# Row norms on VectorE, 24 weight pieces in attention instead of 30, and the first piece loads spread over the loop

## The chip, the cores and the metric

The kernel runs on one core of one Trainium2 chip. The metric is the time of one execution on the device, in microseconds (us). A profiled execution of the same program gives the trace that is read below.

## The reference

Three layers follow one another. Attention has 4 batches, 12 heads, 448 positions and 64 dimensions per head, and uses a sigmoid in place of a softmax. Its output, 1792 rows of 768, goes through a mixture of 8 experts in which each row takes one expert: the choice needs the norm of each row. The last layer multiplies two projections elementwise and projects back.

```python
scores = scale * np.matmul(q, k.transpose(0, 1, 3, 2)) - np.log(S)
x = rows of np.matmul(1.0 / (1.0 + np.exp(-scores)), v)          # 1792 x 768

xn = x / (np.linalg.norm(x, axis=-1, keepdims=True) + 1e-06)
logits = xn @ en.T / tau                                         # 8 experts
expert_idx = np.argmax(logits, axis=1)
out[row] = gate_w[row] * (relu(x[row] @ w1[e]) @ w2[e])          # e = expert_idx[row]

y = (out @ w_a) * (out @ w_b) @ w_out                            # w_a, w_b: 768 x 1536
```

## The kernel before, in words

**Attention** runs over 24 pairs of heads, six per batch, in a software pipeline. Iteration i of the loop (L596) transposes the queries and keys of pair i + 1 on TensorE and splits them into a high and a low part (`tr_pair`: L524 on ScalarE, L525 on VectorE), computes the scores of pair i (L538) with the sigmoid on ScalarE (L539), and multiplies by the values for pair i - 1 (`av_part`, L550). At the end of `av_part` VectorE copies the result to `xT` (L554); this copy also frees the only PSUM buffer of its kind. GpSimd then squares the pair (L559, L562) and adds the square to a sum per batch, `xsq` (L563). `x_tok` (L566) turns pair i - 2 back to rows of tokens: four transposes on TensorE (L573), a copy on VectorE (L574), and after each third pair a store of the rows (L577) on SP's queue.

After a batch's sixth pair `route(b)` is put in a list of background jobs. It multiplies `xT` by the normed expert embeddings `enT` and, in the same group of matmuls, `xsq` by a matrix `sqT` that sums over partitions (L248); ScalarE copies the result (L250), and L254 adds the four quarters with a matrix `sum9`, eight columns for the logits and a ninth for the sum of squares. VectorE takes the ninth as `ss` (L260), and `inv_norm` computes the inverse norm, mostly on GpSimd. `head` (L667) loads tau and the embeddings, norms them and writes `enT`; it is a background job too. `pump` advances one such job by one step (up to its next `yield`), and each iteration has four calls of it. A job that yields True waits for a call that may use PSUM.

**Weight pieces.** The weights of the last layer are made from integer reads of `w_a`, `w_b` and `w_out` in 72 units, six per block f of 128 hidden columns (`prep_load` and `prep_unit`). A unit is 128 x 384: two VectorE instructions (L198, L200), two of ScalarE (L202 and L204, which writes the buffer `ab`), one of GpSimd (L205), and a last one of VectorE (L215). Units of attention are stored to the scratch `wm` (L227). `prep_tick` (L229) stores what is finished, finishes what waits (all but `behind` units), loads the unit three ahead, and starts one unit. There are three buffers `ab`, two `m` and four `raw`. In attention there is one tick at the end of each of the 24 iterations and an extra one with behind=1 in every fourth, so that `6 * F_EARLY` = 30 units are done there. All loads and stores named here are on SP's queue, which issues in program order.

**Experts.** 18 live blocks of 128 rows go through `w1` and `w2`; no unit of weights is made there until its end.

**Last stage** (`glu`). Four groups of up to 512 rows, twelve blocks f each, make 48 steps. Step i first splits the weights of step i + 1 (`w_split`), multiplies (`ab`, L1037 to L1039, with the product of the two projections at L1045 on VectorE), and adds the output of step i - 1. Blocks below `F_EARLY` are loaded from the scratch `wm`; the other blocks of the first group are made in place, with four ticks in even steps and five in odd ones (`prep_more`), and `w_split` forces further ticks while its block lacks units:

```python
while F_EARLY <= i < NF and wr_n.get(i, 0) < 6:
    prep_tick()
```

Of the kernel before, what the change touches and what calls it, by code (L numbers as in the profile page):

```python
# [9 lines left out]
F32 = mybir.dt.float32  # L10
# [5 lines left out]
ALU = mybir.AluOpType  # L16
# [8 lines left out]
def build(ctx: ExitStack, tc: tile.TileContext, q, k, v, emb, tau, w1, w2, wa, wb, wo, out, dbg=None, stop=None):  # L25
# [6 lines left out]
    nc = tc.nc  # L32
    B, H, S, D = q.shape
    E, DM = emb.shape
    DF = w1.shape[2]
    DF2 = wa.shape[1]
    P = 128
    NCH = 4
    CP = S // NCH
    NP = H // 2  # L40
# [3 lines left out]
    HD = DM // 2  # L44
# [28 lines left out]
    def ctile(shape, nm, dt=F32):  # L73
        return const.tile(shape, dt, name=nm, tag=nm)

    ident = ctile([P, P], "ident")
# [11 lines left out]
    bias_s = ctile([P, 1], "bias_s")  # L88
    tau_r = ctile([P, 1], "tau_r")
    enT = ctile([P, KD, 32], "enT")  # L90
    sqT = ctile([P, 32], "sqT")
    sum9 = ctile([P, E + 1], "sum9")
    oh_all = ctile([CP, B * NCH, E], "oh_all")
    rk_all = ctile([CP, B * NCH], "rk_all")
    run = ctile([P, E2], "run")
# [6 lines left out]
    def constants():  # L102
        gp = nc.gpsimd

        def iota(t, pattern, base=0, cm=0):
            gp.iota(t, pattern=pattern, base=base, channel_multiplier=cm, allow_small_or_imprecise_dtypes=True)

        make_identity(nc, ident)
        gp.tensor_copy(out=ident_r, in_=ident)
        gp.memset(bias_s, -math.log(S))  # L110
        gp.memset(enT, 0.0)
        gp.memset(sqT, 0.0)
        gp.memset(sqT[:, E:E + 1], 1.0)
        gp.memset(ones, 1.0)
        gp.affine_select(out=tri, in_=ones, pattern=[[1, P]], compare_op=ALU.is_gt, fill=0.0, base=0,
                         channel_multiplier=-1)
        gp.memset(tri16, 1.0)
        gp.affine_select(out=tri16, in_=tri16, pattern=[[1, E2], [-1, E2]], compare_op=ALU.is_ge, fill=0.0, base=0,
                         channel_multiplier=0)
        iota(iota8m, [[1, E]], base=-E)  # L120
        iota(iota128, [[1, P]])
        iota(ids, [[S, B], [1, NCH]], cm=NCH)
        n0 = len(PHASES[0]) * NCH
        iota(yrow[:, :n0], [[S, len(PHASES[0])], [1, NCH]], base=Y0 + 1, cm=NCH)
        iota(yrow[:, n0:], [[S, len(PHASES[1])], [1, NCH]], base=1, cm=NCH)
        iota(pads, [[P, NBLK]], base=CAP[1] + 1, cm=1)
        iota(blk_i, [[1, NBLK + 1]])
        iota(blk_128, [[P, JMAX]])
        gp.memset(run, 0.0)
        gp.memset(last3, -1.0)  # L130
        gp.tensor_tensor(out=sum9, in0=ident[:, 0:E + 1], in1=ident[:, 32:32 + E + 1], op=ALU.add)
        for g in (2, 3):
            gp.tensor_tensor(out=sum9, in0=sum9, in1=ident[:, 32 * g:32 * g + E + 1], op=ALU.add)

    def inv_norm(ss, rows, cols, tag, eng, res):

# [27 lines left out]

    HU = DM // 2
    units = [(f, part, hf) for f in range(NF) for part in range(3) for hf in range(2)]
    F_EARLY = 5
    next_unit, unit_end = [0], [6 * F_EARLY]
    prep_raw = {}

# [64 lines left out]

    misc = {}
    LATE, END = "late", "end"
    xT, xsq, xtok = {}, {}, {}

    def route(b):  # L240
        ph = phase_of[b]
        c0 = b * NCH

        pl = misc["ps"]()
        ops = [(enT[:, hp, :], xT[b, hp]) for hp in range(NP)] + [(sqT, xsq[b])]
        for i, (l, r) in enumerate(ops):
            g = 32 * (i % 4)
            nc.tensor.matmul(pl[g:g + 32, :S], lhsT=l, rhs=r, start=i < 4, stop=i + 4 >= len(ops))  # L248
        lT = misc["xp"].tile([P, S], F32, tag="lT", name="lT", bufs=1)
        nc.scalar.copy(out=lT, in_=pl[:, :S])  # L250
        yield True
        ps = misc["ps"]()
        for c in range(NCH):
            nc.tensor.matmul(ps[:CP, c * (E + 1):(c + 1) * (E + 1)], lhsT=lT[:, c * CP:(c + 1) * CP], rhs=sum9,  # L254
                             start=True, stop=True)
        ls = small.tile([CP, NCH, E + 1], F32, tag="ls", name="ls")
        nc.vector.tensor_copy(out=ls, in_=ps[:CP, :NCH * (E + 1)].rearrange("p (c e) -> p c e", c=NCH))
        misc[f"logits{b}"] = True
        ss = small.tile([CP, NCH], F32, tag="ss", name="ss")
        nc.vector.tensor_copy(out=ss, in_=ls[:, :, E])  # L260
        res = []
        gp = nc.gpsimd
        yield from inv_norm(ss, CP, NCH, "x", gp, res)
# [4 lines left out]

        ve = nc.vector
        l0 = st("l0")  # L270
        ve.tensor_tensor(out=l0, in0=ls[:, :, :E], in1=rn.unsqueeze(2).to_broadcast([CP, NCH, E]), op=ALU.mult)
        l1 = st("l1")
        ve.tensor_scalar(out=l1, in0=l0, scalar1=tau_r[:CP], scalar2=None, op0=ALU.mult)
        mx = st("mx", (CP, NCH))
# [193 lines left out]
    def attention():  # L468
# [73 lines left out]
        def av_part(i, half):  # L542
            if half == 0:
                av[i] = ps_a.tile([P, 512], F32, tag="av", name="av")
            t = av[i]
            a = A.pop((i, half))
            for c2 in range(2):
                c = 2 * half + c2
                for j in range(2):
                    nc.tensor.matmul(t[j * D:(j + 1) * D, :S], lhsT=raw[i, "v"][:, j, c, :], rhs=a[:, c2, j, :],  # L550
                                     start=c == 0, stop=c == NCH - 1)
            if half == 1:
                x = xT_p.tile([P, S], F32, tag="xT", name="xT", bufs=NP + 1)
                nc.vector.tensor_copy(out=x, in_=t[:, :S])  # L554
                xT[pairs[i]] = x
                b, hp = pairs[i]
                if hp == 0:
                    xsq[b] = xT_p.tile([P, S], F32, tag="xsq", name="xsq", bufs=2)
                    nc.gpsimd.tensor_tensor(out=xsq[b], in0=x, in1=x, op=ALU.mult)  # L559
                else:  # L560
                    x2 = xT_p.tile([P, S], F32, tag="x2", name="x2", bufs=1)
                    nc.gpsimd.tensor_tensor(out=x2, in0=x, in1=x, op=ALU.mult)  # L562
                    nc.gpsimd.tensor_tensor(out=xsq[b], in0=xsq[b], in1=x2, op=ALU.add)  # L563
                del av[i]

        def x_tok(i):  # L566
            b, hp = pairs[i]
            if hp == 0:
                xtok[b] = misc["xp"].tile([CP, NCH, DM], F32, tag="xtok", name="xtok", bufs=1)
            pm = misc["ps"]()  # L570
            pmv = pm[:CP].rearrange("p (c d) -> p c d", c=NCH)
            for c in range(NCH):
                nc.tensor.transpose(out=pmv[:, c, :], in_=xT[b, hp][:, c * CP:(c + 1) * CP], identity=ident)  # L573
            nc.vector.tensor_copy(out=xtok[b][:, :, hp * P:(hp + 1) * P], in_=pmv)  # L574
            if hp % XH == XH - 1:
                ds = slice((hp + 1 - XH) * P, (hp + 1) * P)
                nc.sync.dma_start(out=xs_d[b * S:(b + 1) * S, ds].rearrange("(p c) d -> p c d", c=NCH),  # L577
                                  in_=xtok[b][:, :, ds])
# [11 lines left out]
        load(2, "qk")  # L590
        tr_pair(1)
        bg.append([head(), False, False])
        for u in range(3):
            prep_load(u)
        early_w = None
        for i in range(NPR + 1):  # L596
            if 0 < i and i + 1 < NPR:
                tr_pair(i + 1)
            load(i + 3, "qk")
            load(i + 2, "v")  # L600
            if i < NPR:
                score_half(i, 0)
            if i == NPR:
                one, turn = misc["ps"], [0]

                def either():
                    turn[0] ^= 1
                    return ps_s.tile([P, 2, 512], F32, tag="ps", name="pm2")[:, 0] if turn[0] else one()

                misc["ps"] = either  # L610
            pump((True,))
            if early_w is None and misc.get("flags0"):
                early_w = first_expert()
            if misc.get("tables0") and not misc.get("gathered"):
                gather(0)
                misc["gathered"] = True
            if early_w:
                early_w.pop(0)()
            if 1 <= i <= NPR:
                av_part(i - 1, 0)  # L620
            pump((True,))
            if i < NPR:
                score_half(i, 1)
            pump((LATE,))
            if 1 <= i <= NPR:
                av_part(i - 1, 1)
            if i == NPR:
                both = ps_s.tile([P, 2, 512], F32, tag="ps", name="px0")
                x_load(0, [both[:, hf] for hf in range(2)])
                gather(1)  # L630
            if i >= 2:
                x_tok(i - 2)
                b, hp = pairs[i - 2]
                if hp == NP - 1:
                    routed(b)
            if i < NPR:
                prep_tick(nc.sync)
                if i % 4 == 1:
                    prep_tick(nc.sync, 1)
            pump((END,))  # L640

# [25 lines left out]
    def head():  # L667
# [10 lines left out]
                                       accum_out=sse)  # L678
        res = []
        yield from inv_norm(sse, E, 1, "e", nc.gpsimd, res)  # L680
        nc.vector.tensor_scalar(out=en, in0=emb_sb, scalar1=res[0], scalar2=None, op0=ALU.mult)
        yield True
        pe = misc["ps"]()
# [489 lines left out]
```

## Time and profile before

| | |
|---|---|
| median of 3 runs | 1146.79 us (1141.67 to 1147.87) |
| the profiled execution's own time | 1144.95 us |
| its span | 1142.9 us |
| TensorE busy | 1083.3 us (95%) |
| VectorE busy | 609.5 us (53%) |
| ScalarE busy | 500.7 us (44%) |
| GpSimd busy | 249.4 us (22%) |
| mean granted TensorE clock | 0.981 |
| attention | up to about 250 us |
| experts | about 250 to 600 us |
| last stage | about 600 us to the end |

PE is TensorE's matmuls, PEld its weight loads, DVE VectorE, ACT ScalarE, POOL GpSimd, SP the engine whose queue issues most DMAs; a q behind the name is the engine's queue. Busy times are sums over one execution. A row of a group of instructions gives line, engine, operation, output<-inputs, shapes and count, then the busy time and the mean duration in ns of one, and after the second bar the idle time of the engine just before them with what ended it. A row in order of time gives start and duration in us, and in square brackets the idle time before it and what ended that.

### The profile page before, as it was taken

To read this page: it belongs to the slowest core of one execution; us is meant where nothing else is said; L and a number is where in the kernel's file an instruction comes from. 1 tells how busy PE (TensorE), PEld (TensorE's weight loads), DVE (VectorE), ACT (ScalarE), POOL (GpSimd) and SP (SyncE) were. 2 spreads that over 40 slices of the span, in tenths; PEclk is the share of its full clock that TensorE was granted. 3 is DMA by queue.
4 is the path that set the end of the run, shared out by engine and by line. 5 is a ranking of instruction groups with operands and counts; after the bars stand their busy time and mean duration, and the time that the engine had idled before them with its cause. 6 is when DMAs were issued, how large, how long until landed. Compare 5 with 4: busy or idle time off the path is not lost. (4 is left out here: it accounts for less than half of the span.)

```text
span 1142.9 us, 16747 instructions
## 1 busy us (share of the span) xinstructions
PE 1083.3 (95%) x6004; PEld 876.5 (77%) x6004; DVE 609.5 (53%) x973; ACT 500.7 (44%) x761; POOL 249.4 (22%) x264
## 2 busy tenths in 40 slices
PE   6989898889999999999989789999999999999998
PEld 4545454449998989899877678788888888888997
DVE  2557468775485349453158799733334333333553
ACT  6656565733174438342145555433223233322552
POOL 2545455453122122212113333200000000000000
PEclk9898989999999999999989999999999999999999
DMA  8675758542665467614147765617222072230730
GB/s 183 174 193 145 204 134 229 154 164 100 260 250 188 159 235 263 259 53 147 43 142 265 242 210 167 226 39 301 112 83 83 1 290 83 85 123 1 283 145 28
DMA packets 109544, 184.15 MB, mean 161 GB/s; under 512 B 49656, under 2 KB 81656, under 8 KB 103424
## 3 DMA queue, kind: packets, MB, share of 16 engines
q1 hardware_dynamic: 105472, 167.72, 44.3%
q0 software_dynamic: 3040, 14.94, 3.7%
q8 instruction: 49, 0.80, 0.3%
q14 instruction: 55, 0.45, 0.1%
q10 hardware_dynamic: 928, 0.23, 0.1%
HBM read 150.63 MB, written 32.24 MB: 160 GB/s over the span
## 5 line engine op out<-in xcount | busy, mean ns | idle before, releaser
L1037 PE MATMUL ab<-yh,whi 128*128 128x512 f32 (+1 forms) x576 | 212.3, 368 | 13.3 <-DVE m L1045 7.8
L1038 PE MATMUL ab<-yl,whi 128*128 128x512 f32 (+1 forms) x576 | 210.8, 366 | 0.0
L1039 PE MATMUL ab<-yh,wlo 128*128 128x512 f32 (+1 forms) x576 | 210.5, 365 | 0.0
L1037 PEld LDWEIGHTS ab<-yh,whi 128*128 128x128 f32 x576 | 110.0, 191 | 31.7 <-DVE m L1045 9.7
L1039 PEld LDWEIGHTS ab<-yh,wlo 128*128 128x128 f32 x576 | 109.8, 191 | 17.8
L1038 PEld LDWEIGHTS ab<-yl,whi 128*128 128x128 f32 x576 | 109.8, 191 | 15.9
L1070 PE MATMUL o<-whi,gh 128*128 128x512 f32 x336 | 114.6, 341 | 0.0
L1071 PE MATMUL o<-whi,gl 128*128 128x512 f32 x336 | 113.5, 338 | 0.0
L1072 PE MATMUL o<-wlo,gh 128*128 128x512 f32 x336 | 113.0, 336 | 0.0
L539 ACT ACTIVATE a<-ps,bias_s 112x896 f32<-112x896 f32 x96 | 92.3, 1009 | 35.5 <-PE ps L538 34.7
L205 POOL TENSOR_TENSOR m<-m,raw 128x384 int32<-128x384 int32 x72 | 81.6, 1134 | 119.8 <-DVE m L200 83.9
L730 ACT CAST gh<-m 128x512 fp32r<-128x512 f32 (+1 forms) x48 | 27.3, 569 | 169.9 <-DVE m L1045 169.9
L1045 DVE TENSOR_TENSOR m<-ab,a 128x512 f32<-128x512 f32 (+1 forms) x48 | 29.9, 623 | 134.1 <-PE ab L1039 134.1
L731 DVE TENSOR_TENSOR wlo<-r,whi 128x768 fp32r<-128x768 f32 x70 | 65.5, 990 | 48.6 <-ACT whi L730 48.6
L731 DVE TENSOR_TENSOR wlo<-wx,whi 128x768 fp32r<-128x768 f32 x72 | 67.2, 989 | 43.6 <-ACT whi L730 43.6
L550 PE MATMUL av<-a,v 112*64 112x448 f32 x384 | 87.9, 582 | 0.0
L790 PE MATMUL p<-w1h,xh 128*128 128x512 f32 x216 | 86.3, 399 | 0.1
L792 PE MATMUL p<-w1h,xl 128*128 128x512 f32 x216 | 84.7, 392 | 1.6 <-DVE xl L731 1.6
L791 PE MATMUL p<-w1l,xh 128*128 128x512 f32 x216 | 84.4, 391 | 0.0
L876 PE MATMUL p<-w2h,hTh 128*128 128x384 f32 x288 | 76.2, 345 | 0.0
L793 ACT ACTIVATE h<-p 128x512 f32<-128x512 f32 x34 | 20.4, 601 | 123.6 <-PE p L792 123.6
L921 POOL DMA_INDIRECT ys<-y,idy x18 | 47.4, 2634 | 123.2 <-DVEq L857 71.5
(229 smaller groups left out, 1997.8 us busy)
## 6 DMA issues: line engine op xcount, KB each, us to landing
r<-wm SPq DMA_DIRECT2D x20, 1152.0 KB, 6.3
wx<-wm SPq DMA_DIRECT2D x20, 1152.0 KB, 12.3
r<-in_moe_w_dram SPq DMA_DIRECT2D x28, 768.0 KB, 8.7
r<-in_moe_w_dram SPq DMA_DIRECT2D x18, 1024.0 KB, 7.1
raw<-in_moe_w_a_dram SPq DMA_DIRECT2D x24, 384.0 KB, 3.9
raw<-in_moe_w_b_dram SPq DMA_DIRECT2D x24, 384.0 KB
raw<-in_moe_w_out_dram SPq DMA_DIRECT2D x24, 384.0 KB, 4.5
wm<-ab SPq DMA_DIRECT2D x30, 192.0 KB, 3.8
```

The lines of the kernel that those rows point to most:

```text
L539: nc.scalar.activation(out=a[:, c2], in_=ps[:, :, :S], func=AF.Sigmoid, bias=bias_s[:CP], scale=qscale)
L550: nc.tensor.matmul(t[j * D:(j + 1) * D, :S], lhsT=raw[i, "v"][:, j, c, :], rhs=a[:, c2, j, :], start=c == 0, stop=c == NCH - 1)
L731: eng.tensor_tensor(out=lo, in0=src, in1=f32_hi, op=ALU.subtract)
L790: nc.tensor.matmul(ps, lhsT=xh[:, kk, :], rhs=w1h[kk][:, cs], start=kk == 0, stop=False)
L791: nc.tensor.matmul(ps, lhsT=xh[:, kk, :], rhs=w1l[kk][:, cs], start=False, stop=False)
L792: nc.tensor.matmul(ps, lhsT=xl[:, kk, :], rhs=w1h[kk][:, cs], start=False, stop=kk == KD - 1)
L1037: nc.tensor.matmul(ps[:, :n], lhsT=hi[:, s, cs], rhs=yh[:, kk, :n], start=kk == 0, stop=False)
L1038: nc.tensor.matmul(ps[:, :n], lhsT=hi[:, s, cs], rhs=yl[:, kk, :n], start=False, stop=False)
L1039: nc.tensor.matmul(ps[:, :n], lhsT=lo[:, s, cs], rhs=yh[:, kk, :n], start=False, stop=kk == KD - 1)
L1070: nc.tensor.matmul(t[:, d0:d1], lhsT=gh[:, cs], rhs=hi[:, 2, d0:d1], start=first, stop=False)
L1071: nc.tensor.matmul(t[:, d0:d1], lhsT=gl[:, cs], rhs=hi[:, 2, d0:d1], start=False, stop=False)
L1072: nc.tensor.matmul(t[:, d0:d1], lhsT=gh[:, cs], rhs=lo[:, 2, d0:d1], start=False, stop=last)
```

## The change

The squares on GpSimd and the sum by matmul are gone. In their place `x_tok` squares the turned rows on VectorE: each instruction takes one of the four rows per partition and one half of the 768 columns, 112 x 384, and sums it into one column of `xss`. From the third pair on, each pair squares one row of the first half, and the sixth pair squares all four rows of the second half: eight instructions per batch. `ss` is the sum of the two halves. `route` has one matmul fewer per batch, and `sum9` becomes `sum8`. `F_EARLY` falls from 5 to 4: 24 units in attention and 48 in the last stage. The first three units are loaded at the ends of iterations 0 to 2, ticks begin in iteration 3, and extra ticks stand in iterations 9, 15 and 21. `head` yields six more times before it scales the embeddings.

```diff
-    sqT = ctile([P, 32], "sqT")
-    sum9 = ctile([P, E + 1], "sum9")
+    sum8 = ctile([P, E], "sum8")
...
-    F_EARLY = 5
+    F_EARLY = 4
...
-        ops = [(enT[:, hp, :], xT[b, hp]) for hp in range(NP)] + [(sqT, xsq[b])]
+        ops = [(enT[:, hp, :], xT[b, hp]) for hp in range(NP)]
...
-            nc.tensor.matmul(ps[:CP, c * (E + 1):(c + 1) * (E + 1)], lhsT=lT[:, c * CP:(c + 1) * CP], rhs=sum9,
+            nc.tensor.matmul(ps[:CP, c * E:(c + 1) * E], lhsT=lT[:, c * CP:(c + 1) * CP], rhs=sum8,
...
-        nc.vector.tensor_copy(out=ss, in_=ls[:, :, E])
+        nc.vector.tensor_tensor(out=ss, in0=xss[b][:, 0], in1=xss[b][:, 1], op=ALU.add)
...
-                b, hp = pairs[i]
-                if hp == 0:
-                    xsq[b] = xT_p.tile([P, S], F32, tag="xsq", name="xsq", bufs=2)
-                    nc.gpsimd.tensor_tensor(out=xsq[b], in0=x, in1=x, op=ALU.mult)
-                else:
-                    x2 = xT_p.tile([P, S], F32, tag="x2", name="x2", bufs=1)
-                    nc.gpsimd.tensor_tensor(out=x2, in0=x, in1=x, op=ALU.mult)
-                    nc.gpsimd.tensor_tensor(out=xsq[b], in0=xsq[b], in1=x2, op=ALU.add)
...
+                xss[b] = misc["xp"].tile([CP, 2, NCH], F32, tag="xss", name="xss", bufs=2)
...
+            for hf, c in [(0, hp - XH + 1)] * (hp >= XH - 1) + [(1, c) for c in range(NCH)] * (hp == NP - 1):
+                xc = xtok[b][:, c, hf * HD:(hf + 1) * HD]
+                nc.vector.scalar_tensor_tensor(out=misc["xp"].tile([CP, HD], F32, tag="x2", name="x2", bufs=1),
+                                               in0=xc, scalar=1.0, in1=xc, op0=ALU.mult, op1=ALU.mult,
+                                               accum_out=xss[b][:, hf, c:c + 1])
...
-        for u in range(3):
-            prep_load(u)
...
-            if i < NPR:
+            if i < 3:
+                prep_load(i)
+            elif i < NPR:
                 prep_tick(nc.sync)
-                if i % 4 == 1:
+                if i % 6 == 3 and i > 3:
                     prep_tick(nc.sync, 1)
...
         yield from inv_norm(sse, E, 1, "e", nc.gpsimd, res)
+        for _ in range(6):
+            yield
         nc.vector.tensor_scalar(out=en, in0=emb_sb, scalar1=res[0], scalar2=None, op0=ALU.mult)
```

## Rows read from the trace of the kernel before

**Rows 1.** stages of 50 and 100 us: PE, PEld, DVE, ACT, POOL busy us, granted clock, DMA.

```profile
50.00:100.00 50.00, 43.57 (x284) 24.10 (x282) 26.61 (x44) 28.99 (x39) 24.91 (x29) 0.90 0.66 173
...
600.00:700.00 100.00, 87.60 (x407) 71.73 (x406) 84.95 (x130) 55.47 (x102) 36.03 (x31) 0.97 0.69 227
```

**Rows 2.** VectorE in order of time, attention: the copies of finished pairs.

```profile
27.42 0.60 DVE L554 COPY xT<-av 128x448 f32<-128x448 f32 x1
...
58.31 0.62 DVE L554 COPY xT<-av 128x448 f32<-128x448 f32 x1 [3.28 <-PE av L550]
...
69.65 0.62 DVE L554 COPY xT<-av 128x448 f32<-128x448 f32 x1 [4.57 <-PE av L550]
...
77.13 0.62 DVE L554 COPY xT<-av 128x448 f32<-128x448 f32 x1 [2.81 <-PE av L550]
...
93.62 0.62 DVE L554 COPY xT<-av 128x448 f32<-128x448 f32 x1 [3.79 <-PE av L550]
...
134.68 0.62 DVE L554 COPY xT<-av 128x448 f32<-128x448 f32 x1 [3.27 <-PE av L550]
...
151.38 0.62 DVE L554 COPY xT<-av 128x448 f32<-128x448 f32 x1 [4.05 <-PE av L550]
...
246.52 0.61 DVE L554 COPY xT<-av 128x448 f32<-128x448 f32 x1
```

**Rows 3.** waits up to 420 us: total us, times, longest us.

```profile
ACT ab L204 <- DMA wm<-ab: 31.2, 7, 6.5
```

**Rows 4.** ScalarE in order of time: two of those seven waits.

```profile
62.61 0.56 ACT L204 ACTIVATE ab<-raw 128x384 f32<-128x384 bf16 x1 [3.27 <-DMA wm<-ab]
...
83.69 0.54 ACT L204 ACTIVATE ab<-raw 128x384 f32<-128x384 bf16 x1 [6.43 <-DMA wm<-ab]
```

**Rows 5.** TensorE in order of time: after the second of them.

```profile
87.31 1.66 PE L254 MATMUL pm<-sum,lT 128*112 128x9 f32 x8 [4.19 <-ACT lT L250]
```

**Rows 6.** all engines in order of time: the start.

```profile
15.12 0.46 SPq L670 DMA_DIRECT2D tau_sb<-in_moe_tau_dram  x1
...
19.44 0.17 DVE L675 RECIPROCAL tau_r<-tau_sb 128x1 f32<-128x1 f32 x1 [8.19 <-DMA tau_sb<-in_moe_tau_dram]
...
20.24 1.72 PE L550 MATMUL av<-a,v 112*64 112x448 f32 x8
...
27.55 0.81 PE L685 MATMUL pm<-ident,r 8*128 8x8 f32 x6 [2.22 <-DVE r L681]
```

**Rows 7.** groups of instructions up to 255 us, by line.

```profile
L562 POOL TENSOR_TENSOR x<-xT 128x448 f32<-128x448 f32 x20 | 39.5, 1977 | 64.3 <-DVE xT L554 64.2
...
L200 DVE SCALAR_TENSOR_TENSOR m<-raw,m 128x384 int32<-128x384 int32 x30 | 33.9, 1130 | 1.0
...
L563 POOL TENSOR_TENSOR xsq<-xsq,x 128x448 f32<-128x448 f32 x20 | 26.1, 1305 | 1.6
...
L215 DVE SCALAR_TENSOR_TENSOR ab<-ab,m 128x384 f32<-128x384 f32 x29 | 15.4, 549 | 0.0
```

**Rows 8.** groups of instructions on VectorE, 635 to 770 us, by line.

```profile
L200 DVE SCALAR_TENSOR_TENSOR m<-raw,m 128x384 int32<-128x384 int32 x30 | 16.8, 559 | 1.0
```

**Rows 9.** all engines in order of time: a square with accumulated sum.

```profile
19.71 0.95 DVE L677 SCALAR_TENSOR_TENSOR r<-r 8x768 f32<-8x768 f32 x1
```

**Rows 10.** VectorE in order of time, last stage: one product per step.

```profile
628.70 0.69 DVE L1045 TENSOR_TENSOR m<-ab,a 128x512 f32<-128x512 f32 x1
...
647.54 0.68 DVE L1045 TENSOR_TENSOR m<-ab,a 128x512 f32<-128x512 f32 x1
...
687.89 0.68 DVE L1045 TENSOR_TENSOR m<-ab,a 128x512 f32<-128x512 f32 x1
...
702.97 0.68 DVE L1045 TENSOR_TENSOR m<-ab,a 128x512 f32<-128x512 f32 x1
...
715.86 0.68 DVE L1045 TENSOR_TENSOR m<-ab,a 128x512 f32<-128x512 f32 x1
```

**Rows 11.** ScalarE in order of time, last stage.

```profile
638.40 2.30 ACT L730 CAST whi<-r 128x768 fp32r<-128x768 f32 x3 [2.89 <-DMA r<-wm]
```

More of the change, by code (lines that the diff above doesn't have):

```diff
@@ L111, in constants @@
         gp.memset(enT, 0.0)
-        gp.memset(sqT, 0.0)
-        gp.memset(sqT[:, E:E + 1], 1.0)
         gp.memset(ones, 1.0)
@@ L130, in constants @@
         gp.memset(last3, -1.0)
-        gp.tensor_tensor(out=sum9, in0=ident[:, 0:E + 1], in1=ident[:, 32:32 + E + 1], op=ALU.add)
+        gp.tensor_tensor(out=sum8, in0=ident[:, 0:E], in1=ident[:, 32:32 + E], op=ALU.add)
         for g in (2, 3):
-            gp.tensor_tensor(out=sum9, in0=sum9, in1=ident[:, 32 * g:32 * g + E + 1], op=ALU.add)
+            gp.tensor_tensor(out=sum8, in0=sum8, in1=ident[:, 32 * g:32 * g + E], op=ALU.add)
     def inv_norm(ss, rows, cols, tag, eng, res):
@@ L237, in build @@
     LATE, END = "late", "end"
-    xT, xsq, xtok = {}, {}, {}
+    xT, xss, xtok = {}, {}, {}
     def route(b):
@@ L244, in route @@
         pl = misc["ps"]()
-        ops = [(enT[:, hp, :], xT[b, hp]) for hp in range(NP)] + [(sqT, xsq[b])]
+        ops = [(enT[:, hp, :], xT[b, hp]) for hp in range(NP)]
         for i, (l, r) in enumerate(ops):
             g = 32 * (i % 4)
-            nc.tensor.matmul(pl[g:g + 32, :S], lhsT=l, rhs=r, start=i < 4, stop=i + 4 >= len(ops))
+            nc.tensor.matmul(pl[g:g + 32, :S], lhsT=l, rhs=r, start=i < 4, stop=i + 4 >= NP)
         lT = misc["xp"].tile([P, S], F32, tag="lT", name="lT", bufs=1)
@@ L253, in route @@
         for c in range(NCH):
-            nc.tensor.matmul(ps[:CP, c * (E + 1):(c + 1) * (E + 1)], lhsT=lT[:, c * CP:(c + 1) * CP], rhs=sum9,
+            nc.tensor.matmul(ps[:CP, c * E:(c + 1) * E], lhsT=lT[:, c * CP:(c + 1) * CP], rhs=sum8,
                              start=True, stop=True)
-        ls = small.tile([CP, NCH, E + 1], F32, tag="ls", name="ls")
-        nc.vector.tensor_copy(out=ls, in_=ps[:CP, :NCH * (E + 1)].rearrange("p (c e) -> p c e", c=NCH))
+        ls = small.tile([CP, NCH, E], F32, tag="lgt", name="ls")
+        nc.vector.tensor_copy(out=ls, in_=ps[:CP, :NCH * E].rearrange("p (c e) -> p c e", c=NCH))
         misc[f"logits{b}"] = True
         ss = small.tile([CP, NCH], F32, tag="ss", name="ss")
-        nc.vector.tensor_copy(out=ss, in_=ls[:, :, E])
+        nc.vector.tensor_tensor(out=ss, in0=xss[b][:, 0], in1=xss[b][:, 1], op=ALU.add)
         res = []
@@ L270, in route @@
         l0 = st("l0")
-        ve.tensor_tensor(out=l0, in0=ls[:, :, :E], in1=rn.unsqueeze(2).to_broadcast([CP, NCH, E]), op=ALU.mult)
+        ve.tensor_tensor(out=l0, in0=ls, in1=rn.unsqueeze(2).to_broadcast([CP, NCH, E]), op=ALU.mult)
         l1 = st("l1")
```

## The prediction

> **What bounds the kernel now.** I read the stages first [rows 1]. In attention (the windows up to 250 us) TensorE has gaps: 43.57 of 50 us busy from 50 to 100, at a mean granted clock of 0.90. At the head of the last stage (600 to 700 us) it has gaps too, 87.60 of 100, and there VectorE is the busiest partner, 84.95 of 100. So two places count, and the change touches both.
>
> In attention I then read when VectorE copies out each finished pair [rows 2]. There are 24 copies, the first at 27.42 and the last at 246.52. A quiet iteration takes 77.13 - 69.65 = 7.48 us, and 23 of them would be 172 us; the trace takes 219.1. So 47 us are lost between the copies, and the loss comes in lumps: 58.31 to 69.65 is 11.34, 77.13 to 93.62 is 16.49, 134.68 to 151.38 is 16.70. The waits name the largest cause [rows 3]: ScalarE stands still 31.2 us in seven waits, each at L204, until a buffer `ab` of the weight pieces has been stored. There are three such buffers. An extra tick makes two pieces in one iteration, so its second piece wants a buffer whose store was only just issued; and since the extra tick runs with behind=1, its piece is finished late and two iterations on the next piece wants a buffer stored in the same iteration. Two of the seven [rows 4]: 3.27 us in iteration 5 (an extra tick), 6.43 in iteration 7 (two later). Iteration 7 also ends batch 0, so ScalarE's copy of the logits is late as well, and TensorE waits 4.19 us for it [rows 5]. That the 3.27 us wait stands in an iteration that is 3.86 too long says that such waits reach TensorE one for one.
>
> **The change, part by part.** *Start.* The loads of three weight pieces move from before the loop to the ends of iterations 0 to 2. On SP's queue tau and the embeddings are now issued before them. Before, tau is issued at 15.12 and VectorE stands 8.19 us until 19.44 for it [rows 6]. TensorE ends pair 0 at 20.24 + 1.72 = 21.96, but VectorE, behind tau, the norm of the embeddings and the first weight pieces, copies it only at 27.42 [rows 2, 6]. The ticks of iterations 0 to 2 go, and with them their VectorE, ScalarE and GpSimd work, which stood in front of that copy. The six added yields put the scaling of the embeddings at the end of iteration 2 and their transposes in iteration 3; TensorE's wait of 2.22 us for it [rows 6] goes, and the first user, the routing of batch 0 in iteration 8, covers the delay. The moved loads are needed first in iteration 3, so their time is covered by the loop. Gain: 27.42 - 21.96 = 5.5 us at most, 2.2 us (TensorE's own wait) at least; I take 5.5, as everything in front of that copy but the norm has left.
>
> *Weight pieces in attention.* Before there are 24 ticks and 6 extra ones (iterations 1, 5, 9, 13, 17, 21), 30 pieces; after, 21 and 3 extra (9, 15, 21), 24 pieces. Batches end in iterations 7, 13 and 19. Before, waits fall there (5 + 2, 13, 17 + 2); after, the places of an extra tick are 9, 11, 15, 17, 21, 23, none of them such. Bounds: no wait is left, a gain of 31.2; or all six places wait at the mean of before, 31.2 / 7 = 4.46, so 26.7 remain and the gain is 4.5. Half as many extra ticks gave me the value: half the waits, a gain of 15.6. A reason to go above half: GpSimd's squares stand in front of its part of the weight pieces (L205), which frees the buffers that SP's next load waits for, and SP's stores queue behind that load.
>
> *Squares.* GpSimd loses 44 instructions (4 first squares, 20 later ones, 20 sums): L562 alone is 39.5 us and L563 26.1 [rows 7], all beside other work, nothing on the path. VectorE gains 32 instructions of 112x384 with an accumulated sum, eight per batch, five of them together after a batch's last pair. The nearest rows: L215, the same operation at that width, 0.549 us [rows 7]; the 768-wide square with a sum, 0.95 [rows 9], half of which is 0.47; and L200, 1.130 in attention [rows 7] and 0.559 in the last stage, where no squares run on GpSimd [rows 8]. So an instruction of this form costs 0.47 to 1.13; I take 0.65 (L215 plus 0.1 for reading out the sum, an estimate), 20.8 us in all. Against it VectorE loses six pieces at about 2.19 (priced below), 13.1, and 24 of L200 fall from 1.130 to 0.559, another 13.7. VectorE's sum is 6 us lower, off the path: I cost it at nothing. Its cover is VectorE's idle half (26.61 of 50 busy [rows 1]); at 1.13 the squares would be 36 us and the sum 9 us higher, still under that cover except where five come together.
>
> The trace shows L200 twice as long beside GpSimd's squares. The Trainium skill (SBUF — State Buffer, Who interferes with whom) says why: a VectorE instruction with two SBUF inputs and a GpSimd instruction that reads SBUF take turns on a shared port, and the later one waits for the whole of the earlier. Rows 7 and 8 agree, 1.130 against 0.559 us. By that rule the new squares, with two SBUF inputs, meet what is left on GpSimd too; that is the fourth rival.
>
> *TensorE and small edits.* One matmul of the norms per batch goes, the sums are eight columns wide instead of nine, the norms come from an add of 112x4: 1 us in all at most; I take 1. The last batch's five squares fall into the start of the expert stage, where VectorE has waited for ScalarE's weights, at nothing; if that cover is gone they cost 3.3.
>
> *Last stage.* Six pieces more are made there, 48 instead of 42. Each step has four or five ticks, and the next step's weights must be whole: counting the ticks, one more is forced at the top of steps 7, 8 and 9, where VectorE is the bound. An interval between two products with five pieces is 702.97 - 687.89 = 15.08 us, with four 715.86 - 702.97 = 12.89 [rows 10]: 2.19 per piece. The three forced ones lie on the path, 6.6 us; the rest of the six fall into step 9 and behind, where ticks ran out before and I count on slack. Bounds: 0 to 13.1 (all six). One thing goes: f=4 is now made in place, not loaded. That load ends a wait of 2.89 us [rows 11] in the longest interval, 647.54 - 628.70 = 18.84 [rows 10], a gain of 2.9 (0 if the raw pieces in front of it are late anyway). Net +3.7, bounds -2.9 to +13.1.
>
> **Sum.** -5.5 - 15.6 - 1 + 3.7 = -18.4 us against the profiled execution, 1144.95 (span 1142.9), which is 1126.6. The median, 1146.79, stands 1.84 above that execution, so the forecast is 1128.4.
>
> **Rivals.** *No wait is left* for stored buffers: SP runs ahead of the ticks, as it must have done in iteration 9 before, an extra tick without a wait. -31.2 - 5.5 - 1 + 3.7 = -34.0: 1112.8. Against it: three buffers remain, and the extra tick is the same.
> *The waits move along* to the new places, all six at the mean: -4.5 - 5.5 - 1 + 3.7 = -7.3, and with the start at its lower bound -4.0: 1139.5 to 1142.8. For it: same buffers, same form of tick.
> *The last stage takes it back*: all six pieces on the path (13.1) and four unfinished pieces each waiting about 1.1 us for GpSimd, without the gain at f=4: +17.5 - 22.1 = -4.6: 1142.2. For it: VectorE's 84.95 us there.
> *Slower: the squares hold the stores.* They stand in VectorE's order ahead of L215, which ends a piece; if they run at 1.13 and come five together, L215, the store behind it on SP and ScalarE's L204 are all late, and the six waits are at 6.5, the longest of before: 39 instead of 31.2. 7.8 more there, 6.6 in the last stage with f=4 gaining nothing, less the start's 5.5 and TensorE's 1: +7.9, or 1154.7. It decides from a square of about 1 us. Against it: the extra ticks avoid the iterations with five squares.
> That the change does nothing of what it says would need extra ticks that cost nothing before; the seven waits exclude it.
>
> **Chances.** The forecast 0.47, no wait left 0.15, waits move along 0.18, last stage takes it back 0.12, slower 0.08. What a measurement of this kernel can tell from no change is about 0.5%, 5.7 us. Faster by more: nearly all of the first two, half of the third, a third of the fourth, 0.73. Slower by more: the last and a little of the rest, 0.09. Within: 0.18. The range goes from the second case, 1113, to 1146, which takes in the third and fourth; about 0.05 below and 0.13 above are left out.
>
> **What would show it.** The first copy near 22 us and quiet iterations of 7.5; waits at L204 for stores near 15 us, none in iterations 7, 13 and 19, and these some 6 us shorter; L200 near 0.56 and squares near 0.55 in attention; GpSimd's busy time down by over 70 us; in the last stage three intervals two us longer and no wait of `r<-wm` in step 3. I am wrong if the waits at L204 stay near 27 us, if the squares take over 1 us, or if the last stage loses 10 us or more.

## The result, and the profile after

The changed kernel takes 1114.77 us (median of 4 runs, 1113.61 to 1115.38) against 1145.05 for the kernel before on the same chip: a ratio of 0.9736 with a 95% interval of 0.9704 to 0.9767, faster by 30 us. The forecast was 18.4 us, in a range that reached down to 1113. The measured time lies 2 us above that end. So the sign and the places were right, and the size was too small. The profiled execution took 1113.61 us, its span is 1111.9, TensorE is busy 1070.6 us (96%), VectorE 603.3, ScalarE 500.3 and GpSimd 178.2.

The stages first, with the columns of [rows 1]:

```profile
50.00:100.00 50.00, 50.00 (x352) 27.66 (x349) 31.86 (x80) 36.30 (x49) 11.33 (x21) 1.00 0.75 199
...
600.00:700.00 100.00, 82.49 (x394) 67.32 (x392) 91.33 (x138) 56.28 (x105) 40.02 (x34) 0.98 0.60 200
```

TensorE has no gap left from 50 to 100 us, and its granted clock there is 1.00 instead of 0.90. GpSimd's busy time in it went from 24.91 to 11.33 us. At the head of the last stage VectorE is fuller than before, 91.33 of 100.

The copies of finished pairs, VectorE in order of time, answer to [rows 2] (L551 is L554 of before):

```profile
21.55 0.62 DVE L551 COPY xT<-av 128x448 f32<-128x448 f32 x1 [0.21 <-PE av L547]
...
36.52 0.62 DVE L551 COPY xT<-av 128x448 f32<-128x448 f32 x1 [4.45 <-PE av L547]
...
51.44 0.62 DVE L551 COPY xT<-av 128x448 f32<-128x448 f32 x1 [3.26 <-PE av L547]
58.90 0.62 DVE L551 COPY xT<-av 128x448 f32<-128x448 f32 x1 [3.39 <-PE av L547]
66.36 0.62 DVE L551 COPY xT<-av 128x448 f32<-128x448 f32 x1 [3.39 <-PE av L547]
76.33 0.62 DVE L551 COPY xT<-av 128x448 f32<-128x448 f32 x1 [2.39 <-PE av L547]
...
168.62 0.62 DVE L551 COPY xT<-av 128x448 f32<-128x448 f32 x1 [1.34 <-PE av L547]
...
209.72 0.61 DVE L551 COPY xT<-av 128x448 f32<-128x448 f32 x1
```

The first copy is 5.9 us earlier. The interval that was 11.34 is 58.90 - 51.44 = 7.46, the one that was 16.49 at the end of batch 0 is 76.33 - 66.36 = 9.97. All 23 intervals together take 188.2 us instead of 219.1.

The waits up to 420 us, and the two behind that row in ScalarE's order of time, answer to [rows 3, 4] (L201 is L204 of before):

```profile
ACT ab L201 <- DMA wm<-ab: 6.8, 2, 3.4
```

```profile
103.38 0.56 ACT L201 ACTIVATE ab<-raw 128x384 f32<-128x384 bf16 x1 [3.37 <-DMA wm<-ab]
...
153.73 0.56 ACT L201 ACTIVATE ab<-raw 128x384 f32<-128x384 bf16 x1 [3.43 <-DMA wm<-ab]
```

Of six possible places only iterations 11 and 17 wait, each two behind an extra tick. VectorE's pieces and squares, as groups up to 230 us, answer to [rows 7]:

```profile
L568 DVE SCALAR_TENSOR_TENSOR x<-xtok 112x384 f32<-112x384 f32 x32 | 17.7, 554 | 0.7
...
L197 DVE SCALAR_TENSOR_TENSOR m<-raw,m 128x384 int32<-128x384 int32 x24 | 15.6, 650 | 0.8
...
L212 DVE SCALAR_TENSOR_TENSOR ab<-ab,m 128x384 f32<-128x384 f32 x23 | 12.5, 552 | 0.0
...
L568 DVE DVE_READ_ACCUMULATOR x<-xtok 112x1 f32 x32 | 2.6, 82 | 0.0
```

A square takes 0.554 us and 0.082 for its sum, and L197 (L200 of before) fell from 1.130 to 0.650. The products of the last stage, one per step, answer to [rows 10]; the first and the eleventh of before come first:

```profile
599.68 0.68 DVE L1045 TENSOR_TENSOR m<-ab,a 128x512 f32<-128x512 f32 x1
...
740.02 0.69 DVE L1045 TENSOR_TENSOR m<-ab,a 128x512 f32<-128x512 f32 x1 [4.17 <-PE ab L1039]
```

```profile
564.68 0.69 DVE L1043 TENSOR_TENSOR m<-ab,a 128x512 f32<-128x512 f32 x1
...
593.10 0.68 DVE L1043 TENSOR_TENSOR m<-ab,a 128x512 f32<-128x512 f32 x1
609.16 0.68 DVE L1043 TENSOR_TENSOR m<-ab,a 128x512 f32<-128x512 f32 x1
...
649.39 0.68 DVE L1043 TENSOR_TENSOR m<-ab,a 128x512 f32<-128x512 f32 x1
666.75 0.69 DVE L1043 TENSOR_TENSOR m<-ab,a 128x512 f32<-128x512 f32 x1
681.99 0.68 DVE L1043 TENSOR_TENSOR m<-ab,a 128x512 f32<-128x512 f32 x1
699.35 0.69 DVE L1043 TENSOR_TENSOR m<-ab,a 128x512 f32<-128x512 f32 x1
709.85 0.69 DVE L1043 TENSOR_TENSOR m<-ab,a 128x512 f32<-128x512 f32 x1
```

The third interval is 16.06 instead of 18.84; in it block f=4 is no longer loaded. The three intervals with a forced piece are 17.36, 15.24 and 17.36, where 15.08, 12.89 and 14.81 stood before, so a forced piece costs 2.3 to 2.55 us.

**Where the 31.0 us of span went.** First copy -5.9; the intervals between copies -30.9; from the last copy to the first product of the last stage +1.8; ten intervals between products 145.2 instead of 140.3, +4.8; the rest -0.8. That rest is the next interval, 11.88 instead of 12.66, so the last stage loses 4.0 in all.

### The profile page after: what moved, and what is told of

Read it like the earlier page. It is cut to its first block, busy times and chain, and to the rows that moved or that the text cites. A ratio compares the mean times of both kernels' runs of the same rounds, so it can differ in the third digit from the quotient of the medians.

```text
span 1111.9 us, 16742 instructions
## 1 busy us (share of the span) xinstructions
PE 1070.6 (96%) x5996; PEld 870.6 (78%) x5996; DVE 603.3 (54%) x1037; ACT 500.3 (45%) x761; POOL 178.2 (16%) x218
## 4 chain that ended last, share of the span: by engine, by line
PE 36%; DVE 9%; DMA 3%; issue 2%; ACT 1%; POOLq 0%; POOL 0%; SPq 0%; ACTq 0%; DVEq 0%
PE ab L1035 8%; PE ab L1037 8%; PE ab L1036 8%; PE o L1068 4%; PE o L1069 4%; PE o L1070 4%; DVE wlo L729 3%; DVE m L195 2%; DVE m L197 1%; DVE wx L212 1%; DMA r<-wm 1%; DMA yg<-ys 1%; DVE r L212 1%; DVE m L1043 1%; DVE gl L729 0%
## 5 line engine op out<-in xcount | busy, mean ns | idle before, releaser
L729 DVE TENSOR_TENSOR wlo<-r,whi 128x768 fp32r<-128x768 f32 x70 | 65.7, 993 | 45.8 <-ACT whi L728 45.8
L729 DVE TENSOR_TENSOR wlo<-wx,whi 128x768 fp32r<-128x768 f32 x72 | 67.5, 992 | 42.5 <-ACT whi L728 42.5
L547 PE MATMUL av<-a,v 112*64 112x448 f32 x384 | 82.5, 551 | 0.0
L728 ACT CAST whi<-wx 128x768 fp32r<-128x768 f32 x72 | 55.6, 832 | 42.1 <-PE o L1069 30.2
```

The costliest lines, as they stand in the source:

```text
L728: nc.scalar.copy(out=hi, in_=src)
L729: eng.tensor_tensor(out=lo, in0=src, in1=f32_hi, op=ALU.subtract)
```

## The experiments

The theory of the prediction is that of *waits*: the loss in attention comes from pieces that wait for a stored buffer, so fewer extra ticks at better places bring it back. The rival is that of *squares*: GpSimd's squares, beside which L200 took 1.130 us and without which it took 0.559 [rows 7, 8], hold things up, and the waits only show it. Each ratio below is to the kernel before on the same chip. The medians of that kernel beside these runs lie between 1142.38 and 1145.97 us, so 3 us between the medians of two runs say little by themselves.

**Taking the waits away from the kernel before.** The pieces of extra ticks get a buffer of their own.

```diff
+        ab = (misc["asb"].tile([P, HU], F32, tag="abx", name="abx", bufs=1) if extra else
+              prep_p.tile([P, HU], F32, tag="ab", name="ab", bufs=3))
...
-                    prep_tick(nc.sync, 1)
+                    prep_tick(nc.sync, 1, True)
```

> The kernel before, with a buffer of its own for the pieces of the extra ticks; nothing else changes. Theory of waits (31.2 us of waits at L204 reach TensorE one for one, or more): the waits go, time 1108 to 1118, between copies of pairs some 190 us instead of 219. Theory of squares (GpSimd's squares lengthen VectorE's instructions and hold up the pieces, the waits at L204 are only where it shows): the waits move to other buffers, time 1132 to 1145.

Measured: 1120.92 us, ratio 0.9788 (0.9742 to 0.9833), 25 us faster. The row of waits for stores is gone from its trace. First and last copy:

```profile
27.00 0.60 DVE L555 COPY xT<-av 128x448 f32<-128x448 f32 x1
...
220.33 0.61 DVE L555 COPY xT<-av 128x448 f32<-128x448 f32 x1
```

The intervals take 193.3 us instead of 219.1. So 31.2 us of waits on ScalarE were worth 25 to 26 us of time, and one more buffer, with everything else left in place, brings most of what the change brings. It came 3 us short of the range that one for one would have given. The 3 us are not in waits for stores, which are gone; the last five intervals between copies still take 46.1 us here, and 41.1 in the changed kernel.

**The squares alone.** Schedule, first loads and 30 pieces as before.

```diff
-    F_EARLY = 4
+    F_EARLY = 5
...
+            if i < NPR:
+                prep_tick(nc.sync)
+                if i % 4 == 1:
+                    prep_tick(nc.sync, 1)
```

> The kernel before with the squares on VectorE as in the changed kernel, but with 30 pieces, ticks and first loads as before and no added yields. Theory of waits: the three buffers and six extra ticks are there, so the waits at L204 stay near 30 us, time 1139 to 1148. Theory of squares: the gain beyond the forecast comes from here, waits at L204 below 20 us, time 1125 to 1136.

Measured: 1139.32 us, ratio 0.9947 (0.9923 to 0.997), 6.7 us faster. The waits stay:

```profile
ACT ab L201 <- DMA wm<-ab: 29.0, 7, 6.4
```

So the waits do not come from the squares, as the theory of waits said. But the squares bring some 7 us of their own, of which the forecast had 1; 4.9 of them are in the last five intervals between copies, 45.8 us instead of 50.7.

**The schedule alone.** The changed kernel with the squares and the norms on GpSimd as before.

```diff
-                nc.vector.scalar_tensor_tensor(
...
+                    nc.gpsimd.tensor_tensor(out=x2, in0=x, in1=x, op=ALU.mult)
+                    nc.gpsimd.tensor_tensor(out=xsq[b], in0=xsq[b], in1=x2, op=ALU.add)
```

> The changed kernel with the squares and their sum back on GpSimd and the norms by matmul as before: 24 pieces, the new places of the extra ticks, the spread loads and the added yields remain. Theory of waits: nearly all of the gain, 1114 to 1120, waits at L204 under 12 us. Theory of squares: 1124 to 1132, waits at L204 near 16 us.

Measured: 1122.96 us, ratio 0.9807 (0.9761 to 0.9854). That lies between the two ranges and settles that both parts count: the schedule 23 us, the squares the 8 us between this run and the changed kernel, about what they brought alone. Only one wait for a store is left, 3.7 us, so the squares' share is not in these waits. It is in the end of attention. The copies of pairs 18 and 19 and of the last one, pair 23 (counted from 0):

```profile
170.92 0.62 DVE L554 COPY xT<-av 128x448 f32<-128x448 f32 x1 [1.33 <-PE av L550]
180.03 0.62 DVE L554 COPY xT<-av 128x448 f32<-128x448 f32 x1 [1.95 <-PE av L550]
...
218.68 0.61 DVE L554 COPY xT<-av 128x448 f32<-128x448 f32 x1
```

The five intervals from pair 18 to pair 23 take 218.68 - 170.92 = 47.8 us; in the changed kernel the same five take 209.72 - 168.62 = 41.1 after a copy at 168.62. Two rows of waits of this run, from 171 to 219 us, which the changed kernel has not in this size:

```profile
DVE x_r L161 <- POOL x_ng L157: 2.7, 1, 2.7
...
PE pm L297 <- ACT a L539: 3.0, 1, 3.0
```

VectorE waits for an inverse norm that GpSimd computes among its squares, ScalarE waits for VectorE, TensorE for ScalarE. That makes one of these intervals 10.60 us instead of 7.66. Another is 191.74 - 180.03 = 11.71 instead of 8.62 without any wait for a norm:

```profile
183.16 1.16 DVE L411 TENSOR_SCALAR hotp<-iota,rpf 112x128 f32<-112x128 f32 x1
184.24 1.07 DVE L413 SCALAR_TENSOR_TENSOR hotb<-blk_i,bk,vals 112x84 f32<-112x84 f32 x1
...
185.45 1.60 PE L430 MATMUL pm<-hotb,hotp 112*128 112x84 f32 x8 [1.05 <-DVE hotb L413]
...
189.12 2.56 PE L550 MATMUL av<-a,v 112*64 112x448 f32 x8
```

L411 and L413 fill one of the expert tables; the same two instructions first take 0.28 and 0.30 us there in the changed kernel. Here they are longer, TensorE waits 1.05 us for one of them, and then its multiplication by the values takes 2.56 us instead of 1.72, at a lower granted clock. Over the five intervals that clock is 0.93, and 1.00 in the changed kernel:

```profile
171.00:218.70 47.70, 43.09 (x272) 22.89 (x270) 38.44 (x75) 28.65 (x39) 27.18 (x30) 0.93 0.53 166
```

```profile
168.60:209.70 41.10, 39.74 (x270) 21.59 (x270) 36.40 (x88) 28.54 (x39) 14.16 (x22) 1.00 0.66 201
```

Seven hundredths of 47.7 are 3.3 us, so up to half of the 6.7 (an estimate) is the slower clock behind the gaps.

**The place of the extra ticks.** Three of them as in the changed kernel, but in the iterations that end a batch.

```diff
-                if i % 6 == 3 and i > 3:
+                if i % 6 == 1 and i > 3:
```

> The changed kernel with its three extra ticks in iterations 7, 13 and 19, which end a batch, instead of 9, 15 and 21. Theory of waits, with the place deciding: waits at L204 of 15 to 25 us in and after these iterations, time 1124 to 1134. Theory of squares, in which the place doesn't matter: 1113 to 1118.

Measured: 1130.43 us, ratio 0.9868 (0.9823 to 0.9913), 16 us above the changed kernel.

```profile
ACT ab L201 <- DMA wm<-ab: 19.9, 4, 5.9
```

The same number of extra ticks and of pieces makes 19.9 us of waits instead of 6.8, in four waits instead of two. In the first of them, iteration 7, SP's queue and ScalarE show this order:

```profile
67.72 0.58 SPq L573 DMA_DIRECT2D xs<-xtok  x1
...
71.07 0.41 SPq L224 DMA_DIRECT2D wm<-ab  x1
...
73.34 0.55 ACT L201 ACTIVATE ab<-raw 128x384 f32<-128x384 bf16 x1 [5.85 <-DMA wm<-ab]
```

The row store of the batch (`xs`) stands ahead of the pieces' stores, of which the one at 71.07 is the second, and ScalarE goes on 2.27 us after that one was issued. That the row store is what makes these places bad fits the order, but no run moves it alone. The place decides as much as the number does.

**The start: order of the loads.** The first three loads go back ahead of tau; ticks still begin in iteration 3.

```diff
+        for u in range(3):
+            prep_load(u)
...
-            if i < 3:
-                prep_load(i)
-            elif i < NPR:
+            if 3 <= i < NPR:
```

> The changed kernel with the loads of its first three pieces issued before the loop, ahead of tau, as in the kernel before; ticks still begin in iteration 3. If the order on SP's queue makes the gain at the start: VectorE's wait for tau is near 8 us again, the first copy of a pair at 25 to 27 us instead of 21.6, time 1118 to 1121. If the ticks that left iterations 0 to 2 make it: the first copy at 22 to 23 us, time 1113 to 1117.

Measured: 1117.69 us, ratio 0.9759 (0.9724 to 0.9794). VectorE's wait for tau in the changed kernel and in this run:

```profile
15.60 0.16 DVE L671 RECIPROCAL tau_r<-tau_sb 128x1 f32<-128x1 f32 x1 [4.38 <-DMA tau_sb<-in_moe_tau_dram]
```

```profile
19.64 0.16 DVE L671 RECIPROCAL tau_r<-tau_sb 128x1 f32<-128x1 f32 x1 [8.38 <-DMA tau_sb<-in_moe_tau_dram]
```

It is 8.38 us again. The first copy comes at 24.98, between 21.55 and 27.42. So of the 5.9 us some 3.4 are the order on SP's queue and 2.4 the ticks that left the first iterations. Two copies later the shares are others; the third copy of the kernel before and of this run:

```profile
43.37 0.62 DVE L554 COPY xT<-av 128x448 f32<-128x448 f32 x1 [2.81 <-PE av L550]
```

```profile
38.41 0.62 DVE L551 COPY xT<-av 128x448 f32<-128x448 f32 x1 [4.47 <-PE av L547]
```

Against 36.52 in the changed kernel the order on SP is now worth 1.9 us, and the ticks are worth 5.0: part of what the first copy lost by its late tau is made up. Copy and time both miss the range of the order by a little. Between the medians lie 2.9 us, and the intervals of the two ratios overlap.

**The added yields.** The changed kernel without them.

```diff
-        for _ in range(6):
-            yield
```

> The changed kernel without the six added yields, so that the embeddings are scaled and turned in iteration 1 or 2 as before. If the yields take a wait off the path: TensorE waits 1 to 3 us for the embeddings near 20 to 30 us, time 1115 to 1118. If the earlier tau alone is enough: 1113 to 1116, the first copies of pairs within 0.5 us of the changed kernel's.

Measured: 1115.51 us, ratio 0.9742 (0.9706 to 0.9778), not told apart from the changed kernel. The first copy is at 21.74, and TensorE does not wait for the embeddings. The earlier tau is enough; the yields bring nothing that these runs can see.

**Room on VectorE.** Each square done twice.

```diff
+                for _ in range(2):
+                    nc.vector.scalar_tensor_tensor(
```

> The changed kernel with each of its 32 squares done twice on VectorE, 20 us more work there, 16 of the 32 in the second half of attention. If VectorE has room all through attention: within 3 us of the changed kernel, 1112 to 1118. If VectorE sets the pace in the last six iterations, where only some of the extra squares fall, and where a batch ends: 1119 to 1128, with the last six intervals between copies 3 to 8 us longer in sum.

Measured: 1116.14 us, ratio 0.9766 (0.9745 to 0.9788). Twenty us more work on VectorE cost 1.4 us in the medians and 3 by the ratios, whose intervals overlap. The intervals of its last six iterations are 3.3 us longer, so there the room is small, but the forecast's price for the squares on VectorE, nothing, was near enough. That leaves GpSimd's side.

**GpSimd's work alone.** The changed kernel with GpSimd's 44 instructions put back as idle work that nobody uses.

```diff
+                d = misc["xp"].tile([P, S], F32, tag="d0", name="d0", bufs=1)
+                nc.gpsimd.tensor_tensor(out=d, in0=x, in1=x, op=ALU.mult)
+                if hp > 0:
+                    nc.gpsimd.tensor_tensor(out=d, in0=d, in1=x, op=ALU.add)
```

> The changed kernel with GpSimd's 44 instructions of before put back as idle work whose result nobody uses; the norms still come from VectorE's squares. If GpSimd's work alone made the part of the gain that the forecast lacked (it lengthens VectorE's instructions and stands in GpSimd's queue before the inverse norms): 1119 to 1125, the last six intervals between copies 5 to 8 us longer in sum. If the way the norms reach the routing made it: 1113 to 1117.

Measured: 1123.83 us, ratio 0.981 (0.9747 to 0.9873), 9 us above the changed kernel: the whole share of the squares is back, though nobody waits for their result. The last six intervals take 60.3 us instead of 50.2, more than was expected; the profiled execution is the longest of the four, 1128.29 us. VectorE's groups in this run, up to 250 us:

```profile
L573 DVE SCALAR_TENSOR_TENSOR x<-xtok 112x384 f32<-112x384 f32 x32 | 22.6, 707 | 0.7
...
L212 DVE SCALAR_TENSOR_TENSOR ab<-ab,m 128x384 f32<-128x384 f32 x23 | 22.1, 971 | 0.0
...
L197 DVE SCALAR_TENSOR_TENSOR m<-raw,m 128x384 int32<-128x384 int32 x24 | 18.6, 774 | 0.8
```

The squares go from 0.554 to 0.707 us, and L212, 0.549 to 0.552 in the runs so far, to 0.971, where the idle work meets it. One such meeting, and VectorE's waits for the norms in this run:

```profile
46.47 1.34 POOL L557 TENSOR_TENSOR d<-d,xT 128x448 f32<-128x448 f32 x1
...
46.74 1.49 DVE L212 SCALAR_TENSOR_TENSOR ab<-ab,m 128x384 f32<-128x384 f32 x1
```

```profile
DVE x_r L158 <- POOL x_ng L154: 3.9, 2, 2.6
```

GpSimd's instruction still runs 1.07 us after L212 begins; with L212's own 0.55 that is about its 1.49. The waits for the norms are 3.9 us in two waits, 3.1 in the changed kernel, so the time that a norm spends in GpSimd's queue is not where the 9 us went. Nor is it GpSimd's own part of a piece: VectorE has no idle time before L212 (0.0 in its row), which is what waits for it.

**Contention or queue?** The schedule alone, with the inverse norms on VectorE, so that they are out of GpSimd's queue.

```diff
-        yield from inv_norm(ss, CP, NCH, "x", gp, res)
+        yield from inv_norm(ss, CP, NCH, "x", nc.vector, res)
```

> The run with the schedule alone (squares on GpSimd), with the inverse norms of the rows computed on VectorE instead of GpSimd, so that they don't wait in GpSimd's queue. If that queue is what costs: VectorE's wait for the norms (2.7 us) goes, 3 to 6 us under that run, 1117 to 1120. If the lengthening of VectorE's instructions beside GpSimd costs: within 2 us of it or slower, 1121 to 1126.

Measured: 1123.49 us, ratio 0.9806 (0.9743 to 0.9869), the time of the schedule alone. The wait for the norm is gone and nothing is gained in the time. But the loss only moved: the norms' small instructions now stand on VectorE ahead of a copy, and that interval takes 11.17 us instead of 8.50, the next one 7.81 instead of 10.60. So this run alone does not clear GpSimd's queue. The run with idle squares does better, by its short waits for the norms: what is left there is that VectorE's instructions grow beside GpSimd's, 17.5 us in the three groups shown, and the slower clock behind the gaps.

**A version that beats both.** First the changed kernel with a buffer of its own for extra ticks (the edit of the first experiment):

> The changed kernel with a buffer of its own for the pieces of the extra ticks. Its two waits at L201 for stores (6.8 us) go. Theory of waits, at the price of the first experiment (25 us of time for 31.2 us of waits): 5 us faster, 1108 to 1111. If the remaining waits lie beside other work: 1113 to 1116.

Measured: 1108.08 us, ratio 0.9677 (0.9651 to 0.9704). The last two waits were worth 6.7 us in the medians and 4.5 in the intervals between copies (183.7 us). With that, extra ticks need less distance from one another, and the pieces can come back from the last stage; there are two such buffers now:

```diff
-    F_EARLY = 4
+    F_EARLY = 5
...
-                if i % 6 == 3 and i > 3:
-                    prep_tick(nc.sync, 1)
+                if i in (4, 5, 6, 9, 10, 11, 12, 15, 16):
+                    prep_tick(nc.sync, 1, True)
```

> The changed kernel with 30 pieces in attention again, nine extra ticks in iterations 4, 5, 6, 9, 10, 11, 12, 15 and 16 with two buffers of their own. If the last stage's loss of 4.8 us between its first and eleventh product comes from the six pieces moved there, it is gone, and if attention has the room for them beside TensorE in its quiet iterations: 1103 to 1108. If attention has no room (ScalarE needs 7.1 us of 7.46 in an iteration with two pieces): 1109 to 1118.

Measured: 1104.26 us, ratio 0.9648 (0.962 to 0.9676). Its ten intervals between products take 697.90 - 558.07 = 139.8 us against 145.2: the six pieces' price in the last stage is 5.3 us. In attention six more cost 1.5: the intervals between copies take 185.3 us, against 183.7 in the run with 24 pieces and a buffer of its own. So further, with 36 pieces (extra ticks in iterations 3 to 17, fifteen of them, one more than the expectation says):

```diff
-    F_EARLY = 5
+    F_EARLY = 6
...
+                if i < 18:
+                    prep_tick(nc.sync, 1, True)
```

> The changed kernel with 36 pieces in attention, extra ticks in iterations 4 to 17 and two buffers of their own for them, so 36 in the last stage. If a piece costs nothing in attention's quiet iterations and 2.2 us in the last stage, as the run with 30 pieces showed: 4 to 9 us under that run, 1096 to 1101. If the iterations that end a batch, or ScalarE, have no room for a second piece: 1103 to 1110.

Measured: 1096.95 us, ratio 0.9601 (0.9582 to 0.962), 18 us under the changed kernel. The intervals between copies take 187.6 us, so twelve more pieces cost attention 3.8 us, and the ten between products fall to 130.0. A stage of 50 us in attention, columns as above:

```profile
100.00:150.00 50.00, 49.28 (x347) 27.41 (x347) 44.76 (x101) 39.98 (x60) 17.84 (x27) 1.00 0.97 264
```

TensorE is as full as in the changed kernel (48.51 us there), while VectorE reaches 44.76 of 50 and the DMA engines 0.97. Whether still more pieces fit was not tried.

## Why the prediction was right, and where it was too small

*Start, -5.5.* Measured -5.9 at the first copy, by the working given: tau earlier, no ticks in front of the copy; at the third it is 36.52 - 43.37, -6.9. The part on the yields was empty.

*Waits, -15.6.* This term was mis-sized. Half the extra ticks were taken to leave half the waits; 6.8 of 31.2 us are left. The count of places was right, but not what makes a place wait: with the batch ends free, only two of six do, and with the same three ticks at the batch ends 19.9 us remain. At the price that the first experiment gave (25 us of time for 31.2 us of waits) the 24.4 us that went are about 20 us. "One for one" was a little high, and near the truth by luck, for a wait does not reach TensorE whole. Behind the 3.27 us in iteration 5 of the kernel before, TensorE shows this, and its granted clock from 65.5 to 67.5 us is 0.50, the lower of its two levels, 1.2 GHz:

```profile
60.05 0.36 PE L538 MATMUL ps<-qkl,qkh 64*112 64x448 f32 x2
...
64.92 0.66 PE L538 MATMUL ps<-qkh 64*112 64x448 f32 x2 [2.24 <-ACT a L539]
65.37 0.58 PE L538 MATMUL ps<-qkh,qkl 64*112 64x448 f32 x2
```

```profile
65.50:67.50 2.00, 2.00 (x14) 1.19 (x12) 0.00 (x0) 1.29 (x3) 0.00 (x0) 0.50 0.86 239
```

The wait leaves a gap of 2.24 us, and the matmuls behind it run at 0.58 us instead of 0.36; the two together make the 3.86. It is the same in iteration 7: 4.19 us of gap [rows 5] for 6.43 of wait, in an iteration 6.5 us longer than the changed kernel's. The prediction read the clock of 0.90 and gave it no term; its price per wait held it unseen.

*Squares, nothing on the path.* This step failed, and on the side that I did not look at. What VectorE takes on is nearly free, as costed: squares of 0.55 us, and doubling them costs 1.4 us. What GpSimd gives up was called nothing too, because it lay beside other work. It is worth 7 to 9 us: 6.7 alone, 8 on top of the schedule, 9 when put back as idle work. The prediction had its mechanism in hand, L200 at 1.130 beside GpSimd and 0.559 without, booked it as 13.7 us of VectorE time, and hid it behind VectorE's mean idle share. In the last five intervals, where the expert tables and the first weights of the experts fall in, VectorE is busy 36.40 of 41.1 us even in the changed kernel, so that cover is nearly gone.

That GpSimd's work alone lengthens VectorE's is what the Trainium skill states (SBUF — State Buffer, Who interferes with whom): a VectorE instruction with two SBUF inputs contends with a GpSimd instruction that reads SBUF, over ports that it calls an exclusive lock. The run with idle squares agrees, L212 at 0.971 against 0.552 us. That this port is the cause of all of the 9 us is argued, not shown, since no run keeps GpSimd busy without reading SBUF.

*TensorE and small edits, -1.* Too small to be seen.

*Last stage, +3.7.* Measured +4.8 over ten intervals and +4.0 with the eleventh: forced pieces at 2.3 to 2.55 each where 2.19 was written, 2.8 us back at f=4 where 2.9 was, 0.6 back in the second interval, and the tenth 1.2 longer, most of which the eleventh gives back.

*Rivals.* "No wait is left" gave 1112.8 and came nearest in time, for another reason: two waits are left, and the squares make up the rest. "The waits move along" fell with the two waits, "the last stage takes it back" with +4.8, "the squares hold the stores" with squares at 0.554 us. The 1.8 us between the last copy and the last stage stay open: TensorE's wait for `xl` at the start of the expert stage is 0.8 us longer, and the runs with 30 and 36 pieces, which have the same squares, do not show the rest.

## What to carry to other kernels

When a producer is run twice in one turn, count how many turns its buffer is held, and look for what stands ahead of its release on an in-order queue: one more buffer, or another turn, was worth 16 to 25 us here. An engine off the critical path is not free to use: price its work also by how much longer its neighbour's instructions become beside it, and in the stretch where that neighbour is fullest, not at its mean. Price a gap on TensorE with the slower clock behind it: 2.24 us of gap cost 3.86 here. A tight last stage can be relieved by an early one for as long as the early one's bound, here TensorE, stays full.

## What the runs showed that I had not expected

TensorE's granted clock from 50 to 100 us was 0.90 with the gaps and is 1.00 without them: behind a gap its matmuls took 0.58 us instead of 0.36, so a gap also costs some time after it. Attention took twelve more pieces for 3.8 us of path: 187.6 us between first and last copy with 36 pieces, 183.7 with 24, both with buffers of their own for extra ticks. And a square with two SBUF inputs and an accumulated sum runs at the rate of the plain form, 0.554 against 0.552 us at equal width. The Trainium skill (Vector Engine (DVE) Microarchitecture Reference, Points that are easy to get wrong) says that this family of instructions halves its throughput with two SBUF sources that are not bf16; the plain form here has two such sources too, so these rows show no cost of accumulating beyond the 0.082 us for reading the sum out, and do not test a halving against a form with one source.
